# Query tiles transposed by VectorE in 32x32 blocks instead of by TensorE, tokens of a tile in another order, logits copied by ScalarE

## The chip, the cores and the metric

The kernel runs on one core of a Trainium2 chip. The core has five engines, each of which runs its own program in order: TensorE (PE, matrix products, with its weight loads shown as PEld), VectorE (DVE), ScalarE (ACT), GpSimd (POOL) and SyncE (SP, which here only issues DMAs). They meet through semaphores. Data are moved by 16 DMA engines. The metric is the device time of one execution in microseconds (us), smaller being better.

## The reference: what is computed

A multi-query attention (8 batches, 16 query heads, one key and value head, 384 tokens, head size 64) whose output, reshaped to 3072 tokens of 1024, goes through a mixture of experts with two levels of gates: a group of four, and in it one of four experts. Each token is handled by one expert of 16.

```python
scores = scale * np.matmul(q, k.transpose(0, 1, 3, 2))
attn = softmax(scores)                       # over the keys
x = np.matmul(attn, v)                       # -> (8*384, 16*64)
g_idx = np.argmax(x @ w_group, axis=1)
# for each group g and expert e of it:
e_idx = np.argmax(xg @ w_expert[g], axis=1)
h = np.maximum(xg[mask_e] @ w1[g, e], 0.0)
ye = h @ w2[g, e]
out[tok_idx] = (g_w * e_w)[:, None] * ye
```

With the inputs used, all 384 tokens of a batch go to one expert in seven batches; in the last batch 363 go to one and 21 to another.

## The kernel before

**Tiles and slots.** The 384 tokens of a batch are three tiles of 128 tokens; there are 24 tiles. In the kernel before, partition p of tile j holds token 3p + j. The 16 heads of a tile are eight pairs, called units. One pass of the main loop (`for i in range(NSL)`) is here called a slot. A slot handles two units, so a tile has 4 slots and a batch 12, and the loop has 96. The order of the work is written out by hand: nothing is rescheduled, each engine gets its instructions in the order in which the Python code issues them. `at(slot, where, fn)` puts a step into a slot, and `run(i, where)` calls it at that place of the slot.

**One slot**, in the order of issue: the scores of two units on PE (L161, two heads beside each other in the array, 8 matmuls; the scores fill both buffers of the pool `ps_s`); `soft`: for each unit the negated row maxima on DVE (L169, `nmx`) and two exponentials on ACT (L172, `pr`); then, in the first two slots of a tile (p = 0 and 1), small matmuls and groups of the expert's matmuls (`advance`), and in the last two (p = 2 and 3) half of the product with v of the tile before (L209); the places "v" and "m2"; two transposes on DVE in blocks of 32x32 (L193, into `ring`) of the probabilities of two slots before; the place "w"; the reciprocals of the row sums on DVE (L183, `rinv`), by which POOL scales the probabilities (L187); the place "g", where loads are issued. L209 reads the whole ring of a tile, and the last transposes of a tile stand in slot p = 1 of the next.

**Queries.** `load_q` brings a tile as 128 tokens x 16 heads x 64 by one DMA on SP, into one of three buffers. `q_group` turns four head pairs with four PE transposes against an identity (L147) into a bank of PSUM, which ACT copies to `qt` (L151). The second half of a tile is turned in its own slot p = 0, the first half of the next in slot p = 1.

**Gates.** After the attention of a tile, its logits are a matmul (L230, place "m2" of slot p = 0), copied to `lt` (L239, place "w"), summed by a second matmul in the next slot (L247) and copied to `lg` (L251, place "v"). `gate_masks` (L267 to L284, DVE and one exponential on ACT) runs behind the lg copy, also in "v", twice for a batch: for its first tile and for the other two. Slots are counted here from the first of the batch whose gates are meant, so that the numbers run on into the next batch's scores: lg copies stand in slots 9, 13 and 17 and the masks in 9 and 17. In slot 9 a small matmul (L294, `gate_choose`) counts the first tile's choices, from which the batch's expert is picked (`gate_pick`, slot 10), and its weights are loaded by POOL (L394).

**Experts.** The expert of a batch is 14 groups of 8 matmuls and an eviction: eight of the first layer (L419, evicted by ACT at L425 to `h_t`) and six of the second (L433, evicted at L451 to `y`). They are spread over slots p = 0 and 1 of the next batch: two groups in a slot, three in most slots p = 1, from slot 17 on. The three tiles of y are stored by SP (L476). The last batch has a second expert, whose results are stored in halves (L492). At the end a loop would handle any further pairs of batch and expert; there is none with these inputs.

Of the kernel before, what the change touches and what calls it, by code (L numbers as in the profile page):

```python
# [9 lines left out]
FP32 = mybir.dt.float32  # L10
BF16 = mybir.dt.bfloat16
I32 = mybir.dt.int32
P = 128
AX = mybir.AxisListType
ALU = mybir.AluOpType
# [4 lines left out]
def kernel(  # L20
# [11 lines left out]
    nc = tc.nc  # L32
# [15 lines left out]


    xb_dram = nc.dram_tensor("xb_scratch", [B, P, KO * S], BF16).ap()  # L50
    out_v = out.rearrange("(b p j) d -> b p j d", p=P, j=ST)
    w1f = moe_w1.rearrange("g e (ko ki) f -> (g e) ki ko f", ki=P)
    w2f = moe_w2.rearrange("g e (fo fi) d -> (g e) fi fo d", fi=P)

# [29 lines left out]
    ring = singles.tile([P, 3, 4, 2, S], FP32)  # L84
    NB = S // 32

    def xbank():
        x = ps_x.tile([P, 512], FP32, tag="x", name="x")
        return x
# [5 lines left out]

    def load_q(t, first=False):
        b, j = t // ST, t % ST
        q_sb = qpool.tile([P, H, D], FP32, tag="q", bufs=3)
        qv = q[b].rearrange("h (p j) d -> p j h d", j=ST)
        if first:  # L100
            nc.sync.dma_start(out=q_sb[:, 0:H // 4, :], in_=qv[:, j, 0:H // 4, :])
            nc.scalar.dma_start(out=q_sb[:, H // 4:H // 2, :], in_=qv[:, j, H // 4:H // 2, :])
            nc.sync.dma_start(out=q_sb[:, H // 2:H, :], in_=qv[:, j, H // 2:H, :])
        else:
            nc.sync.dma_start(out=q_sb[:], in_=qv[:, j, :, :])
        st["q", t] = q_sb

    def load_k(b, first=False):
# [29 lines left out]
    def q_group(t, half, parts=1):  # L138
        q_sb = st["q", t]
        half ^= swapped(t)  # L140
        qt = pool.tile([P, 512], FP32, tag="qt", bufs=3)
        n = 4 // parts
        for part in range(parts):
            pt = xbank()
            for c in range(part * n, (part + 1) * n):
                h = 2 * (half * 4 + c)
                nc.tensor.transpose(  # L147
                    out=pt[:, ts(c, P)], in_=q_sb[:, h:h + 2, :].rearrange("p t d -> p (t d)"), identity=ident[:]
                )
            r = slice(part * n * P, (part + 1) * n * P)  # L150
            nc.scalar.copy(out=qt[:, r], in_=pt[:, r])  # L151
        st["qt", t, half] = qt

    def scores(u):
# [26 lines left out]
    def norm(us):  # L181
        rinv = ppool.tile([P, 2, 2], FP32, tag="rinv")
        nc.vector.reciprocal(out=rinv[:], in_=st.pop(("ssum", us[0]))[:])  # L183
        for k, u in enumerate(us):
            for h in range(2):
                pr = st["pr", u][:, h, :]
                nc.gpsimd.tensor_scalar(  # L187
                    out=pr, in0=pr, scalar1=rinv[:, k, h:h + 1], scalar2=1.0, op0=ALU.mult, op1=ALU.mult
                )
# [46 lines left out]

    def logits_out(b, j):
        lt = pool.tile([P, P], FP32, tag="lt")
        nc.vector.tensor_copy(out=lt[:], in_=st.pop(("lt_ps", b, j))[:, 0:P])  # L239
        if j == 0:  # L240
            st["lg", b] = pool.tile([P, ST, NL], FP32, tag="lg", name="lg")
        st["lt", b, j] = lt
# [5 lines left out]
        st["l_ps", b, j] = l_ps  # L248

    def logits2_out(b, j):  # L250
        nc.vector.tensor_copy(out=st["lg", b][:, j, :], in_=st.pop(("l_ps", b, j))[:, 0:NL])  # L251


    NG = ST * (1 + G)
# [216 lines left out]
    def main_expert(b, on_act):  # L471
        w1, w2 = st.pop(("w", b))

        def store(j, y):
            if b < B - 1:
                nc.sync.dma_start(out=out_v[b, :, j, :], in_=y[:])  # L476
            else:
                st["y", j] = y

        yield from expert(st["xb", b], w1, w2, scaled(lambda: st["gsel", b][0], store), any_bank, on_act)  # L480

    def second_expert(on_act):

        b = B - 1

        def result(j, nh, yp, by_act):
            y = st["y", j]
            nc.vector.scalar_tensor_tensor(
                out=y[:, ts(nh, 512)], in0=yp, scalar=st["gsel", b][1][:, j:j + 1], in1=y[:, ts(nh, 512)],
                op0=ALU.mult, op1=ALU.add,  # L490
            )
            nc.sync.dma_start(out=out_v[b, :, j, ts(nh, 512)], in_=y[:, ts(nh, 512)])  # L492

        yield from expert(st["xb", b], *st.pop("w_second"), result, any_bank, on_act)

# [20 lines left out]
    def at(slot, where, fn, *args):  # L516
        later.setdefault((slot, where), []).append((fn, args))

    def run(slot, where):
        for fn, args in later.pop((slot, where), []):  # L520
            fn(*args)
# [36 lines left out]
            at(s0 + 8, "m0", prep_batch, b + 1)  # L558
            at(s0 + 8, "v", prep_out, b + 1)
    for t in range(NT):  # L560
        at(4 * t, "m1", q_group, t, 1)
        if t + 1 < NT:
            at(4 * t + 1, "m1", q_group, t + 1, 0)
        if 1 <= t < NT - 2:
            at(4 * t, "g", load_q, t + 2)

    load_k(0, first=True)
# [31 lines left out]
    busy(1)  # L599
    q_group(0, 0, 2)  # L600
    load_v(0)
    load_q(2)
    for i in range(NSL):
        t, p = i // 4, i % 4
        if i >= SB + 5 and (i - 5) % SB == 0:
            pending.append(main_expert((i - 5) // SB - 1, lambda k: True))
        us = (2 * i, 2 * i + 1)
        for u in us:
            scores(u)
        run(i, "s")  # L610
        soft(us, lambda: run(i, "b"))
        if p < 2:
            run(i, "m0")
            advance(1)
            run(i, "m1")
            advance(2 if p == 1 and t % ST > 0 else 1)
        elif t > 0:
            pv(t - 1, (p - 2) * NB // 2, (p - 1) * NB // 2)
        run(i, "v")
        run(i, "m2")  # L620
        if i >= 2:
            transp(2 * i - 4)
            transp(2 * i - 3)
        run(i, "w")
        norm(us)
        if p == 3 and t > 0:
            pv_out(t - 1)
        run(i, "g")
# [79 lines left out]
    with tc.For_i(0, n_rem, 1) as it:  # L708
        free.clear()
        e = nc.gpsimd.value_load(lse[0:1, ds(it, 1)], min_val=0, max_val=GE - 1)  # L710
        w1, w2 = load_w(e, 0), load_w(e, 1)
        bi = nc.sync.value_load(lsb[0:1, ds(it, 1)], min_val=0, max_val=B - 1)
        xr = pool.tile([P, KO, S], BF16, tag="xb", name="xr", bufs=2)
        nc.sync.dma_start(
            out=xr[:].rearrange("p c t -> p (c t)"), in_=xb_dram[ds(bi, 1)].rearrange("o p c -> (o p) c")
        )
        pid = nc.vector.value_load(lsi[0:1, ds(it, 1)], min_val=0, max_val=NP - 1)
        gcol = pool.tile([P, ST], FP32, tag="gcol")
        nc.vector.tensor_copy(out=gcol[:], in_=grem_all[:, ds(pid, 1), :].rearrange("p o j -> p (o j)"))
        bp = nc.gpsimd.value_load(lsb[0:1, ds(it, 1)], min_val=0, max_val=B - 1)  # L720

        def add(j, y):
            nc.gpsimd.dma_start(
                out=out_v[ds(bp, 1), :, j, :].rearrange("o p d -> (o p) d"), in_=y[:], accum_op=ALU.add
            )

        for _ in expert(xr, w1, w2, scaled(lambda: gcol, add), bank_end):
            pass
# [30 lines left out]
```

## Time and profile before

| | |
|---|---|
| median of 3 runs | 558.66 us (555.86 to 561.7) |
| profiled execution | 560.02 us, span of the profile 558.6 us |
| PE busy | 530.6 us, 95% of the span |
| DVE busy | 418.4 us, 75% |
| ACT busy | 339.2 us, 61% |
| POOL busy | 270.6 us, 48% |
| PE transposes of queries (L147) | 192, 29.5 us busy |
| their copies on ACT (L151) | 49, 29.0 us busy, 0.60 us for one of 128x512 |
| lt copies on DVE (L239) | 24, 6.7 us busy, 31.7 us of waiting ahead of them |
| lg copies on DVE (L251) | 24, 4.0 us busy |

The page is one profiled execution. A row of its groups names the line, the engine, the operation, and what is written from what, with the shape; behind it the busy time, the mean of one in ns, and the idle time of the engine ahead of it with what ended that. The chain is followed back from the last instruction to whatever released it, so its shares say which engine's work sets the end. In a timeline the first two numbers are start and length in us; "x4" says that several instructions are merged. The granted clock is the share of full speed that PE's clock was given.

### The profile page before, as it was taken

How to read it: one execution, taken by the hardware profiler on the slowest of the kernel's cores; microseconds unless marked ns; L12 is line 12 of the kernel's file. 1: busy time of each engine (PE TensorE's matmuls, PEld its weight loads, DVE VectorE, ACT ScalarE, POOL GpSimd, SP SyncE). 2: the span in 40 equal slices, each digit the busy share in tenths (PEclk: the TensorE clock that was granted, in tenths of full speed). 3: DMA queues.
4: the chain of work that ended last, by engine and by line, in shares of the span. 5: the costliest groups of instructions: out<-in, count | busy, mean ns of one | idle time of the engine just before them, and what ended most of it. 6: DMA issues, size and time to landing. Idle time of an engine off the chain costs nothing.

```text
span 558.6 us, 17530 instructions
## 1 busy us (share of the span) xinstructions
PE 530.6 (95%) x7074; PEld 310.1 (56%) x7074; DVE 418.4 (75%) x847; ACT 339.2 (61%) x1043; POOL 270.6 (48%) x456
## 2 busy tenths in 40 slices
PE   7598899999999999999999999999999999979994
PEld 3255456655665556655665556655665555555452
DVE  4989988877888778877888678876888778823322
ACT  4776666666666666766666676676666676613210
POOL 2655954564457444565447535555447535622000
PEclk9999999999999999999999999999999999989999
DMA  7710993099805993099706992199706960299923
GB/s 118 161 30 13 177 229 75 2 195 233 202 2 97 210 250 77 4 200 247 181 1 111 213 262 48 11 211 247 164 2 111 213 189 2 29 212 263 222 51 115
DMA packets 98098, 75.15 MB, mean 135 GB/s; under 512 B 75104, under 2 KB 75104, under 8 KB 98016
## 3 DMA queue, kind: packets, MB, share of 16 engines
q0 software_dynamic: 19008, 37.75, 38.1%
q1 hardware_dynamic: 78080, 36.04, 24.7%
q8 instruction: 57, 0.93, 0.7%
q10 hardware_dynamic: 928, 0.23, 0.2%
q14 instruction: 25, 0.20, 0.1%
HBM read 92.88 MB, written 18.87 MB: 200 GB/s over the span
## 4 chain that ended last, share of the span: by engine, by line
PE 88%; DVE 6%; ACT 3%; issue 2%; ACTq 0%; DVEq 0%
PE x L209 24%; PE s L161 22%; PE x L419 13%; PE x L433 11%; PE sb L433 6%; PE sb L419 4%; PE x L147 3%; DVE nmx L169 3%; ACT pr L172 3%; PE x L230 2%; DVE ring L193 2%; PE x L247 1%; PE x L94 1%; PE x L129 0%; PE x L338 0%
## 5 line engine op out<-in xcount | busy, mean ns | idle before, releaser
L187 POOL TENSOR_SCALAR pr<-pr,rinv 128x384 f32<-128x384 f32 x384 | 218.2, 591 | 222.6 <-DVE rinv L183 222.6
L172 ACT ACTIVATE pr<-s,nmx 128x384 f32<-128x384 f32 x384 | 217.9, 580 | 139.6 <-DVE nmx L169 133.1
L169 DVE TENSOR_REDUCE nmx<-s 128x2 f32<-128x768 f32 x192 | 174.4, 948 | 58.0 <-PE s L161 57.8
L193 DVE STREAM_TRANSPOSE ring<-pr 128x768 f32<-128x768 f32 x192 | 175.4, 952 | 0.0
L161 PE MATMUL s<-kt,qt 64*128 64x384 f32 x768 | 152.8, 511 | 13.0 <-ACT pr L172 12.8
L209 PE MATMUL x<-ring,v_sb 32*64 32x256 f32 x4608 | 142.5, 382 | 5.8 <-issue 4.8
L209 PEld LDWEIGHTS x<-ring,v_sb 32*64 32x64 f32 x4608 | 103.5, 132 | 47.8 <-issue 28.9
L161 PEld LDWEIGHTS s<-kt,qt 64*128 64x128 f32 x768 | 65.1, 186 | 71.5 <-ACT pr L172 37.3
L419 PE MATMUL x<-xb,w 128*128 128x384 bf16 x448 | 79.5, 326 | 0.0
L172 ACT ACTIVATION_READ_ACCUMULATOR pr<-s,nmx 128x1 f32 x384 | 77.9, 203 | 0.0
L419 PEld LDWEIGHTS <-w 128*128 128x128 bf16 x576 | 56.6, 100 | 32.0
L433 PEld LDWEIGHTS <-h_t 128*128 128x128 bf16 x432 | 41.3, 100 | 50.4 <-issue 9.1
L433 PE MATMUL x<-w,h_t 128*128 128x512 bf16 x288 | 68.2, 379 | 0.0
L222 ACT COPY xt<-x 128x256 f32<-128x256 f32 x96 | 29.1, 391 | 13.5 <-PE x L209 13.1
L425 ACT ACTIVATE h_t<-x 128x384 bf16<-128x384 f32 x56 | 28.2, 506 | 9.4 <-PE x L419 8.8
L433 PE MATMUL sb<-w,h_t 128*128 128x512 bf16 x144 | 33.2, 388 | 0.0
L394 POOL DMA_DIRECT2D w<-in_moe_w_dram x36 | 27.5, 777 | 10.5 <-PE x L247 5.6
L151 ACT COPY qt<-x 128x512 f32<-128x512 f32 (+1 forms) x49 | 29.0, 594 | 2.7 <-PE x L147 2.7
L239 DVE COPY lt<-x 128x128 f32<-128x128 f32 x24 | 6.7, 278 | 31.7 <-PE x L230 31.6
L147 PE MATMUL x<-ident,q_sb 128*128 128x128 f32 x192 | 29.5, 277 | 0.0
L147 PEld LDWEIGHTS x<-ident,q_sb 128*128 128x128 f32 x192 | 23.7, 143 | 8.9 <-issue 1.6
L223 POOL CAST xb<-xt 128x1024 bf16<-128x1024 f32 x24 | 24.9, 1040 | 7.5 <-ACT xt L222 7.5
(83 smaller groups left out, 217.5 us busy)
## 6 DMA issues: line engine op xcount, KB each, us to landing
w<-in_moe_w_dram POOLq DMA_DIRECT2D x36, 1024.0 KB, 18.7
q_sb<-in_q_dram SPq DMA_DIRECT2D x23, 512.0 KB, 6.4
out_dram<-y SPq DMA_DIRECT2D x21, 512.0 KB, 8.3
xb_scratch<-xb SPq DMA_DIRECT2D x8, 768.0 KB, 5.5
v_sb<-in_v_dram SPq DMA_DIRECT2D x32, 96.0 KB, 4.2
out_dram<-y SPq DMA_DIRECT2D x6, 256.0 KB, 2.0
kk<-in_k_dram SPq DMA_DIRECT2D x15, 96.0 KB, 5.4
q_sb<-in_q_dram SPq DMA_DIRECT2D x1, 256.0 KB, 4.1
```

Source lines behind the costliest of these rows:

```text
L147: nc.tensor.transpose(out=pt[:, ts(c, P)], in_=q_sb[:, h:h + 2, :].rearrange("p t d -> p (t d)"), identity=ident[:])
L151: nc.scalar.copy(out=qt[:, r], in_=pt[:, r])
L161: nc.tensor.matmul(out=s[:, h, 0:S], lhsT=qt[r, ts(cc, P)], rhs=kt[r, :], start=True, stop=True)
L169: nc.vector.tensor_reduce(out=nmx[:], in_=s[:, :, 0:S], axis=AX.X, op=ALU.max, negate=True)
L172: nc.scalar.activation(out=pr[:, h, :], in_=s[:, h, 0:S], func=ACTF.Exp, bias=nmx[:, h:h + 1], scale=1.0, accum_out=ssum[:, k, h:h + 1],)
L187: nc.gpsimd.tensor_scalar(out=pr, in0=pr, scalar1=rinv[:, k, h:h + 1], scalar2=1.0, op0=ALU.mult, op1=ALU.mult)
L193: nc.vector.transpose(out=ring[:, (u // 4) % 3, u % 4].rearrange("p h s -> p (h s)"), in_=st.pop(("pr", u))[:].rearrange("p h s -> p (h s)"),)
L209: nc.tensor.matmul(out=o[i][h * D:(h + 1) * D, 0:2 * P].rearrange("d (g c q) -> d g c q", g=2, c=4), lhsT=v_sb[r, n, :], rhs=ring[r, a:z + ...
L222: nc.scalar.copy(out=xt[:, :, ts(i, 32)], in_=o[:, 0:2 * P].rearrange("p (c q) -> p c q", c=KO))
L419: nc.tensor.matmul(out=hp[:, 0:S], lhsT=w1[:, ko, ts(fc, P)], rhs=xb[:, ko, :], start=(ko == 0), stop=(ko == KO - 1))
L425: nc.scalar.activation(out=h_t[:, fc, :], in_=hp[:, 0:S], func=ACTF.Relu)
L433: nc.tensor.matmul(out=yp, lhsT=h_t[:, fo, ts(j, P)], rhs=w2[:, fo, ts(nh, 512)], start=(fo == 0), stop=(fo == FO - 1),)
```

## The change

Five things are changed together.

- Which 128 tokens make a tile, and where they stand: tile j is now tokens 128j to 128j + 127, and partition 32n + r holds token 128j + 4r + n. The stores of the result follow: their destination has the dimensions n, r and d. Keys and values are as before.
- Tiles 0 to 4 are still turned by PE, but loaded in four DMAs, one for each n (tile 0 in eight, half of them on ACT's queue).
- Tiles 5 to 23 are loaded in four DMAs, one for each half of the 64 elements of each of two heads of a pair, with runs of 224 elements, of which blocks of 32 in every 64 are used. A new function, `q_blocks`, turns four pairs in one 32x32 block transpose on DVE, straight into `qt`. It stands at a new place "e", behind the reciprocals of the slot, in the same slots as `q_group`.
- The buffers of the queries are two of 2048 elements in each partition instead of three of 1024. The load of tile 2 moves from ahead of the loop to slot 0.
- The copies to `lt` and `lg` are issued to ACT instead of DVE, at the same places.

```diff
--- before.py
+++ after.py
@@ -48,7 +48,8 @@
 
 
     xb_dram = nc.dram_tensor("xb_scratch", [B, P, KO * S], BF16).ap()
-    out_v = out.rearrange("(b p j) d -> b p j d", p=P, j=ST)
+    QN = P // 32
+    out_v = out.rearrange("(b j r n) d -> b j n r d", j=ST, n=QN, r=32)
     w1f = moe_w1.rearrange("g e (ko ki) f -> (g e) ki ko f", ki=P)
     w2f = moe_w2.rearrange("g e (fo fi) d -> (g e) fi fo d", fi=P)
 
@@ -84,6 +85,8 @@
     ring = singles.tile([P, 3, 4, 2, S], FP32)
     NB = S // 32
 
+    TQ = 5
+
     def xbank():
         x = ps_x.tile([P, 512], FP32, tag="x", name="x")
         return x
@@ -95,14 +98,25 @@
 
     def load_q(t, first=False):
         b, j = t // ST, t % ST
-        q_sb = qpool.tile([P, H, D], FP32, tag="q", bufs=3)
-        qv = q[b].rearrange("h (p j) d -> p j h d", j=ST)
-        if first:
-            nc.sync.dma_start(out=q_sb[:, 0:H // 4, :], in_=qv[:, j, 0:H // 4, :])
-            nc.scalar.dma_start(out=q_sb[:, H // 4:H // 2, :], in_=qv[:, j, H // 4:H // 2, :])
-            nc.sync.dma_start(out=q_sb[:, H // 2:H, :], in_=qv[:, j, H // 2:H, :])
+        q_sb = qpool.tile([P, 2 * H * D], FP32, tag="q", bufs=2)
+        if t < TQ:
+            q_sb = q_sb[:, 0:H * D].rearrange("p (h d) -> p h d", h=H)
+            qv = q[b].rearrange("h (j r n) d -> j n r h d", n=QN, r=32)
+            for h0 in range(0, H, H // 2 if first else H):
+                for n in range(QN):
+                    (nc.scalar if first and n % 2 else nc.sync).dma_start(
+                        out=q_sb[32 * n:32 * (n + 1), h0:h0 + (H // 2 if first else H), :],
+                        in_=qv[j, n, :, h0:h0 + (H // 2 if first else H), :],
+                    )
         else:
-            nc.sync.dma_start(out=q_sb[:], in_=qv[:, j, :, :])
+
+            q_sb = q_sb[:].rearrange("p (c x) -> p c x", c=H // 2)
+            qv = q[b].rearrange("(c h) (j r n) d -> h j r c (n d)", h=2, n=QN, r=32)
+            for i in range(4):
+                nc.sync.dma_start(
+                    out=q_sb[32 * i:32 * (i + 1), :, 0:QN * D - 32],
+                    in_=qv[i // 2, j, :, :, 32 * (i % 2):32 * (i % 2) + QN * D - 32],
+                )
         st["q", t] = q_sb
 
     def load_k(b, first=False):
@@ -149,6 +163,14 @@
                 )
             r = slice(part * n * P, (part + 1) * n * P)
             nc.scalar.copy(out=qt[:, r], in_=pt[:, r])
+        st["qt", t, half] = qt
+
+    def q_blocks(t, half):
+
+        half ^= swapped(t)
+        qt = pool.tile([P, 512], FP32, tag="qt", bufs=3)
+        q_sb = st["q", t][:, 4 * half:4 * (half + 1), :].rearrange("p c (n d) -> p (c n) d", n=QN)
+        nc.vector.transpose(out=qt[:].rearrange("p (x d) -> p x d", d=32), in_=q_sb[:, :, 0:32])
         st["qt", t, half] = qt
 
     def scores(u):
@@ -236,7 +258,7 @@
 
     def logits_out(b, j):
         lt = pool.tile([P, P], FP32, tag="lt")
-        nc.vector.tensor_copy(out=lt[:], in_=st.pop(("lt_ps", b, j))[:, 0:P])
+        nc.scalar.copy(out=lt[:], in_=st.pop(("lt_ps", b, j))[:, 0:P])
         if j == 0:
             st["lg", b] = pool.tile([P, ST, NL], FP32, tag="lg", name="lg")
         st["lt", b, j] = lt
@@ -248,7 +270,7 @@
         st["l_ps", b, j] = l_ps
 
     def logits2_out(b, j):
-        nc.vector.tensor_copy(out=st["lg", b][:, j, :], in_=st.pop(("l_ps", b, j))[:, 0:NL])
+        nc.scalar.copy(out=st["lg", b][:, j, :], in_=st.pop(("l_ps", b, j))[:, 0:NL])
 
 
     NG = ST * (1 + G)
@@ -473,7 +495,7 @@
 
         def store(j, y):
             if b < B - 1:
-                nc.sync.dma_start(out=out_v[b, :, j, :], in_=y[:])
+                nc.sync.dma_start(out=out_v[b, j], in_=y[:])
             else:
                 st["y", j] = y
 
@@ -489,7 +511,7 @@
                 out=y[:, ts(nh, 512)], in0=yp, scalar=st["gsel", b][1][:, j:j + 1], in1=y[:, ts(nh, 512)],
                 op0=ALU.mult, op1=ALU.add,
             )
-            nc.sync.dma_start(out=out_v[b, :, j, ts(nh, 512)], in_=y[:, ts(nh, 512)])
+            nc.sync.dma_start(out=out_v[b, j, :, :, ts(nh, 512)], in_=y[:, ts(nh, 512)])
 
         yield from expert(st["xb", b], *st.pop("w_second"), result, any_bank, on_act)
 
@@ -558,10 +580,12 @@
             at(s0 + 8, "m0", prep_batch, b + 1)
             at(s0 + 8, "v", prep_out, b + 1)
     for t in range(NT):
-        at(4 * t, "m1", q_group, t, 1)
-        if t + 1 < NT:
-            at(4 * t + 1, "m1", q_group, t + 1, 0)
-        if 1 <= t < NT - 2:
+        for x, u, half in ((4 * t, t, 1), (4 * t + 1, t + 1, 0)):
+            if u < TQ:
+                at(x, "m1", q_group, u, half)
+            elif u < NT:
+                at(x, "e", q_blocks, u, half)
+        if t < NT - 2:
             at(4 * t, "g", load_q, t + 2)
 
     load_k(0, first=True)
@@ -599,7 +623,6 @@
     busy(1)
     q_group(0, 0, 2)
     load_v(0)
-    load_q(2)
     for i in range(NSL):
         t, p = i // 4, i % 4
         if i >= SB + 5 and (i - 5) % SB == 0:
@@ -623,6 +646,7 @@
             transp(2 * i - 3)
         run(i, "w")
         norm(us)
+        run(i, "e")
         if p == 3 and t > 0:
             pv_out(t - 1)
         run(i, "g")
@@ -721,7 +745,7 @@
 
         def add(j, y):
             nc.gpsimd.dma_start(
-                out=out_v[ds(bp, 1), :, j, :].rearrange("o p d -> (o p) d"), in_=y[:], accum_op=ALU.add
+                out=out_v[ds(bp, 1), j].rearrange("o n r d -> (o n) r d"), in_=y[:], accum_op=ALU.add
             )
 
         for _ in expert(xr, w1, w2, scaled(lambda: gcol, add), bank_end):
```

## The prediction

> **What bounds the kernel now.** I read the profile page first (parts 1, 2 and 4), then the chain in order of time, then the timeline of the same stretch.
>
> ```profile
> PE 530.6 (95%) x7074; PEld 310.1 (56%) x7074; DVE 418.4 (75%) x847; ACT 339.2 (61%) x1043; POOL 270.6 (48%) x456
> ...
> PE 88%; DVE 6%; ACT 3%; issue 2%; ACTq 0%; DVEq 0%
> ```
>
> TensorE (PE) carries 88% of the chain that ended last. A slot, one pass of the loop over two head pairs, looks so in the chain (start, length, what):
>
> ```profile
> 262.71 1.49 PE s L161 x8
> 264.20 0.34 PE x L247 x2
> 264.54 1.30 PE x L419 x8
> 265.84 0.44 PE x L147 x4
> 266.28 2.60 PE x L419 x16
> 268.88 1.49 PE s L161 x8
> 270.37 2.78 PE x L209 x96
> 273.15 1.49 PE s L161 x8
> ```
>
> From scores to scores PE does not wait. The four query transposes (L147) are 0.44 us on it. The other engines in this slot (a gate slot, the 18th of a batch):
>
> ```profile
> 265.35 0.17 DVE L251 COPY lg<-x 128x20 f32<-128x20 f32 x1
> 265.55 0.20 DVE L267 TENSOR_REDUCE mx<-lg 128x10 f32<-128x40 f32 x1
> ...
> 266.89 1.83 DVE L193 STREAM_TRANSPOSE ring<-pr 128x768 f32<-128x768 f32 x2
> ...
> 268.92 0.49 ACT L425 ACTIVATE h_t<-x 128x384 bf16<-128x384 f32 x1 [0.65 <-PE x L419]
> ...
> 269.77 1.82 DVE L169 TENSOR_REDUCE nmx<-s 128x2 f32<-128x768 f32 x2 [1.00 <-PE s L161]
> ...
> 270.83 0.58 ACT L172 ACTIVATE pr<-s,nmx 128x384 f32<-128x384 f32 x1 [1.29 <-DVE nmx L169]
> ```
>
> VectorE (DVE) copies lg as soon as PE has it and goes straight on to the gates and to the ring, which PE's L209 needs next. ScalarE (ACT) ends the slot only after PE's last expert matmul: its third h_t starts at 268.92, 0.04 us behind it.
>
> **What goes.** 19 of 24 tiles lose two groups of L147: 38 x 0.44 = **-16.7 us**, all on the chain. ACT loses 38 copies of 0.60 us, off the path.
>
> **What comes on DVE.** 38 block transposes of 128x512. The nearest row, the ring's, moves 128x768 at a pitch of 0.91: 0.61 by size, 0.63 taken. The source is read in runs of 32 elements, which no row shows: 1.27 is the upper bound (half rate), 0.49 the lower (half the 0.95 of a ring instruction). They stand behind rinv and ahead of the next maxima. In a slot without gates DVE then has 1.82 + 1.83 + 0.14 + 0.63 = 4.4 us in a PE slot of 5.3 to 5.7: covered. PE waits for none, as the scores use the result two slots later or at the next tile. DVE loses the 24 lt copies, which held it waiting for PE; in the first tiles, where DVE is on the chain, I count -0.8 in all.
>
> **What moves: the lg copy.** The lt copy on ACT costs nothing: ACT idles 1.8 us there before its next exponentials. The lg copy does. In ACT's program it stands behind the slot's four exponentials and its expert evictions, three in a gate slot, and the third waits for PE's last matmul. DVE is in order, so its gate reduction L267 now waits for that, and the ring transposes, rinv, the block transpose and the next maxima wait behind it. This happens in slots 9 and 17 of a batch (counted from 0); the other lg copies have no early reader.
>
> Slot 17, in the times above: PE's fill ends at 268.44. Third h_t 268.48 to 268.97; lg copy about 0.2 (the 128x20 exponential on ACT took 0.22) to 269.17; L267 at 269.25 instead of 265.55; gates 1.34 (265.55 to 266.89); ring 270.59 to 272.42. PE has finished its scores at 269.93 and L209 waits until 272.56: **2.63 us idle**. DVE: rinv and block transpose to 273.19, then maxima; exponentials 1.06 after their start, at 274.25. Early in the trace, where PE waits for score banks, scores start 1.29 and 2.41 us after the first exponential (8.75 to 10.04 and 11.16). So the next scores start at 275.54 and 276.66, L209 runs to 280.19, and the following scores end at 281.68 instead of 278.90: 2.78 late with the 0.44 already credited, **3.2 us** gross. Seven times: +22.4.
>
> Slot 9: PE's own gate_choose matmul (L294) needs the mask. Fill ends 288.94; lg done 289.67; mask 290.9; L294 at 291.1, **2.15 us idle** on PE; scores to 292.73; ring to 292.72; maxima 293.6; exponentials 294.68; scores 295.97 and 297.09; then gate_pick (0.91) on DVE; scores of the next tile end at 302.50 instead of 299.53, 3.4 gross. ACT is then so late that two evictions and the lt copy end at 308.6, where PE wants lt at 308.1: 0.6 more. **4.0 us**, seven times: +28.0. In batch 0 slot 9 has no expert: lg would come at 45.9 instead of 43.7, +1.9.
>
> **Ends.** Tile 0 arrives in eight DMAs on two queues; the last of its first half is issued about 0.8 us later than now (SP takes 0.8 for one): +0.6. load_q(2) moves past SP's small loads into slot 0 and lands (6.4 us median) long before slot 5. Each later tile is four issues on SP instead of one, and with two buffers it waits for the tile's second block transpose; four slots (20 us) remain against 6.4 (21.3 at most): nothing counted. In the tail lg waits behind an eviction: +0.5.
>
> Sum so far: -16.7 + 22.4 + 28.0 + 1.9 - 0.8 + 1.1 = **+35.9**.
>
> **The clock.** PE's idle stretches have a second price. Columns: stretch, length, PE busy, ..., granted clock, DMA share, GB/s.
>
> ```profile
> 13.12:16.54 3.42, 1.83 (x8) 0.60 (x8) 1.95 (x4) 2.81 (x10) 2.25 (x5) 1.00 0.82 186
> ...
> 494.40:497.82 3.42, 1.43 (x47) 0.93 (x32) 0.00 (x0) 0.00 (x0) 1.27 (x2) 1.00 1.08 270
> 497.82:504.64 6.82, 5.89 (x63) 3.30 (x63) 0.00 (x0) 1.29 (x4) 1.04 (x1) 0.50 1.12 212
> ```
>
> After 3.42 us with 1.99 idle the clock was halved for 6.82 us; after 3.42 with 1.59 idle it was not. I read this as a fixed grid of 3.41 us and a limit between, 1.8. An idle 2.63 puts 1.8 into one interval from 72% of the starting points, 2.15 from 57%: 7 x 0.72 + 7 x 0.57 = 9 halvings. In slot 17 one makes L209 and the scores take twice their time until about 279.3, and the following scores end some 2.8 us later: 25. Part is given back where PE would have waited anyway: 0.4 and 0.6 in slot 9's sum, and 0.7 in slot 8, where DVE has 6.1 us against PE's 5.4, 1.7 x 7 = 12. **+13.5.**
>
> The Trainium skill (TensorE: Matmul & The Clock Gate, Part 1: The HAM clock gate) says the clock halves after at least one idle window of about 3.4 us. A 2.6 us wait alone would then do nothing and the time would be that of the rival without halvings. The row above, halved after 1.43 us of work in the window, speaks against it.
>
> Total +49.4 on the profiled execution's 560.02 us (span 558.6 and 1.4 around it), which is 1.4 above the median of 558.66: **608 us**.
>
> **Rivals.**
> - *No halvings*: +35.9, 594.5 us. For it: one row carries the price. Chance 0.22.
> - *The output stores become narrow*: the destination was one dimension of 128 rows and is now 4 x 32. In the last 15 us a 256 KB store takes 0.74 us at a DMA share of 0.92, 0.74 x 0.92 x 16 = 10.9 us of one engine. On 4 engines that is 2.7, six stores one behind the other from 544.63 end 16.3 later instead of at 552.28: +8.7, 617 us. No row shows such a store. The Trainium skill (DMA: Bandwidth & Descriptors, Why a DMA increments its semaphore by 16 and not by 1) says that the number of engines must divide the slowest dimension of both sides, which gives 4 here. Chance 0.20.
> - *Dear block transposes* (1.27): +0.64 in 14 chains and as much in slot 8 seven times, +13, 621 us. Chance 0.08.
> - *Faster*: the gates wait less than thought. The two stalls pay for the gain as soon as one costs 16.7 / 14 = 1.2 us; if DVE's lg came before ACT's evictions, only -16.7 and small terms stay: 542 us. Against it: both engines run their programs in order, and the eviction ahead of lg ends after PE's fill. Chance 0.05.
> - *The new token order changes the routing*: from the inputs, seven batches send all 384 tokens to one expert and the last 363 and 21 to two, so the first tile picks the same in either order. A further expert would be 20.8 us (520.43 to 541.19). With late query loads: 0.03.
>
> The forecast itself has 0.42. Range **590 to 622**: from no halvings with cheap transposes (-2) and 2 of noise, to narrow stores with a few halvings more. A difference under 1% can't be told from none in this kernel. Faster by over 1% 0.05, within 1% 0.02, slower 0.93.
>
> **What would show it.** Right: L267 waits 14 times for ACT's lg, 3 to 4 us each; L209 waits for the ring; granted clock below 0.97; slots of plain tiles 0.44 shorter; block transposes near 0.63. Wrong: L267 starting right behind the second maximum, or a PE that stays busy through slots 9 and 17.

## The result: slower, 611.7 us

The changed kernel takes **611.7 us** (median of 6 runs, 607.67 to 612.79) against 557.64 us for the kernel before, now also of 6 runs: a ratio of 1.0946, 95% interval 1.0894 to 1.0997. Its profiled execution took 608.54 us, its span is 607.0 us against 558.6, and the mean granted clock is 0.964 against 0.991. The time is 3.7 us above the forecast of 608 and inside the range. The sum behind the forecast was less right than its end: it priced the main loop 14.8 us too high and the tail 14.1 us too low. The experiments below show where.

From the page of the changed kernel, its engines, the chain by engine, two groups and the weights' loads:

```profile
PE 532.5 (88%) x6900; PEld 302.4 (50%) x6922; DVE 430.2 (71%) x837; ACT 328.5 (54%) x1053; POOL 269.9 (44%) x456
...
PE 62%; DMA 12%; DVE 10%; ACT 6%; issue 4%; POOL 2%; SPq 1%; POOLq 0%; DVEq 0%; ACTq 0%
...
L289 DVE TENSOR_REDUCE mx<-lg 128x5 f32<-128x20 f32 (+1 forms) x16 | 3.0, 185 | 68.6 <-ACT lg L273 68.6
...
L173 DVE STREAM_TRANSPOSE qt<-q_sb 128x512 f32<-128x512 f32 x38 | 26.0, 683 | 0.0
...
w<-in_moe_w_dram POOLq DMA_DIRECT2D x36, 1024.0 KB, 21.9
```

PE has 152 weight loads fewer, those of the query transposes, and is busy a little longer all the same, as a part of its work ran at half clock. Its share of the chain fell from 88% to 62%. Two things took its place. DVE's gate reduction (L289, formerly L267) waits 68.6 us for ACT's copy of lg, which was expected; and 12% of the chain is now DMA (7% loads of weights, 5% loads of keys), which was not: the median weight load takes 21.9 us from issue to landing instead of 18.7. The block transposes take 683 ns each.

The chain of the changed kernel in slot 17 of a batch, the place that the prediction worked out (start, length, what):

```profile
416.39 3.90 PE x L441 x24
420.29 1.49 PE s L183 x8
421.78 2.41 issue
424.19 3.18 PE x L231 x94
427.37 1.64 PE s L183 x8
```

There is no L161 (formerly L147) left, and PE stands still for 2.41 us between the scores and the product with v. The timeline of the same place, ACT, DVE and PE, says why:

```profile
420.33 0.49 ACT L447 ACTIVATE h_t<-x 128x384 bf16<-128x384 f32 x1 [0.70 <-PE x L441]
420.71 0.17 ACT L273 COPY lg<-x 128x20 f32<-128x20 f32 x1
420.92 0.20 DVE L289 TENSOR_REDUCE mx<-lg 128x10 f32<-128x40 f32 x1 [3.64 <-ACT lg L273]
...
422.25 1.83 DVE L215 STREAM_TRANSPOSE ring<-pr 128x768 f32<-128x768 f32 x2
...
424.07 0.68 DVE L173 STREAM_TRANSPOSE qt<-q_sb 128x512 f32<-128x512 f32 x1
424.19 0.68 PE L231 MATMUL x<-ring,v_sb 32*64 32x256 f32 x8 [2.41 <-issue]
```

PE had lg's matmul ready at 416.39. ACT copies it at 420.71, behind the third eviction (L447), which waits for PE's last expert matmul. DVE has waited 3.64 us; gates and ring follow, and L231 starts when the ring is done. The list of waits of the whole execution (in total, times, longest):

```profile
DVE mx L289 <- ACT lg L273: 68.6, 16, 17.1
...
PE x L316 <- DVE g_mask L306: 15.8, 8, 2.7
```

One of the 16 waits, of 17.1 us, lies in the tail; the other 15 have a mean of (68.6 - 17.1) / 15 = 3.4 us.

To see where the time went, I take the span apart at two points: the first scores, and the first scores of the last slot.

| us | first scores | loop | tail | span |
|---|---|---|---|---|
| before | 6.79 | 474.2 | 77.6 | 558.6 |
| after | 7.14 | 507.7 | 92.2 | 607.0 |
| difference | +0.35 | +33.5 | +14.6 | +48.4 |

The tail, that is everything behind the start of the last slot's scores, lost 14.6 us, where the prediction counted 0.5. Its waits for DMAs in the changed kernel:

```profile
ACT y L473 <- DMA out_dram<-y: 3.6, 1, 3.6
...
PEld L441 <- DMA w<-in_moe_w_dram: 3.5, 1, 3.5
PE sb L441 <- DMA w<-in_moe_w_dram: 3.2, 1, 3.2
PE sb L455 <- DMA w<-in_moe_w_dram: 3.0, 1, 3.0
```

The kernel before had none of these. PE waits twice: at 555.86 for the second-layer weights of the last batch's expert, at 571.10 for the first-layer weights of the second expert (the PEld row is the same wait as the PE row below it). With each wait the clock is halved for 3.41 us, from 556.67 and from 570.32. The load behind the second wait is the longest piece of the chain:

```profile
527.02 44.03 DMA w<-in_moe_w_dram
```

In the kernel before the same load took 30.5 us, and PE did not wait for it. And when DVE has written the last result at 593.45, the output is not nearly out. The windows of the changed kernel at that point, while results still come and after the last one (stretch, length, PE, PEld, DVE, ACT, POOL, granted clock, DMA share, GB/s):

```profile
586.00:593.50 7.50, 6.66 (x31) 2.84 (x29) 3.54 (x5) 0.00 (x0) 0.00 (x0) 1.00 0.25 78
594.00:604.00 10.00, 0.00 (x0) 0.00 (x0) 0.00 (x0) 0.00 (x0) 0.00 (x0) 0.68 0.25 95
```

and the same stretch of the kernel before, up to its last result:

```profile
545.00:552.40 7.40, 6.55 (x31) 2.75 (x29) 3.43 (x5) 0.00 (x0) 0.00 (x0) 1.00 0.41 158
```

The DMA share stands at 0.25, as much as four engines of 16, for 17 us. The last six stores are 768 packets with a mean of 93 ns; they take 18.0 us from the first packet to the last, so 768 x 0.093 / 18.0 = 4.0 engines work on the average. From 586 us on, exactly four packets are under way for 12.2 us of 18.2; in the kernel before, the last stores have up to 16 at a time. This is the rival of the narrow stores, and the Trainium skill's rule that the prediction cited for it (DMA: Bandwidth & Descriptors, Why a DMA increments its semaphore by 16 and not by 1) agrees with these rows.

### The profile page after: what moved, and what is told of

Its sections match the earlier page's. It is cut to its first block, busy times and chain, and to the rows that moved or that the text cites. A ratio compares the mean times of both kernels' runs of the same rounds, so it can differ in the third digit from the quotient of the medians.

```text
span 607.0 us, 17318 instructions
## 1 busy us (share of the span) xinstructions
PE 532.5 (88%) x6900; PEld 302.4 (50%) x6922; DVE 430.2 (71%) x837; ACT 328.5 (54%) x1053; POOL 269.9 (44%) x456
## 4 chain that ended last, share of the span: by engine, by line
PE 62%; DMA 12%; DVE 10%; ACT 6%; issue 4%; POOL 2%; SPq 1%; POOLq 0%; DVEq 0%; ACTq 0%
PE x L231 19%; PE s L183 17%; PE x L441 10%; PE x L455 9%; DMA w<-in_moe_w_dram 7%; DMA kk<-in_k_dram 5%; ACT pr L194 5%; DVE nmx L191 4%; DVE ring L215 3%; PE sb L441 2%; PE sb L455 2%; PE x L252 2%; POOL pr L209 1%; PE x L269 1%; SPq L125 1%
## 5 line engine op out<-in xcount | busy, mean ns | idle before, releaser
L183 PE MATMUL s<-kt,qt 64*128 64x384 f32 x768 | 158.0, 521 | 13.6 <-ACT pr L194 12.4
L231 PE MATMUL x<-ring,v_sb 32*64 32x256 f32 x4608 | 151.1, 397 | 20.7 <-issue 16.8
L231 PEld LDWEIGHTS x<-ring,v_sb 32*64 32x64 f32 x4608 | 113.1, 138 | 63.5 <-issue 48.3
L441 PE MATMUL x<-xb,w 128*128 128x384 bf16 x448 | 76.2, 326 | 0.0
L455 PE MATMUL x<-w,h_t 128*128 128x512 bf16 x270 | 64.3, 380 | 0.9
L289 DVE TENSOR_REDUCE mx<-lg 128x5 f32<-128x20 f32 (+1 forms) x16 | 3.0, 185 | 68.6 <-ACT lg L273 68.6
L447 ACT ACTIVATE h_t<-x 128x384 bf16<-128x384 f32 x56 | 26.0, 500 | 10.2 <-PE x L441 9.6
L473 ACT ACTIVATE y<-x,gsel 128x512 f32<-128x512 f32 x36 | 24.2, 696 | 3.7 <-PE x L455 3.7
L173 DVE STREAM_TRANSPOSE qt<-q_sb 128x512 f32<-128x512 f32 x38 | 26.0, 683 | 0.0
L441 PE MATMUL sb<-xb,w 128*128 128x384 bf16 x128 | 22.9, 339 | 3.2 <-DMA w<-in_moe_w_dram 3.2
## 6 DMA issues: line engine op xcount, KB each, us to landing
w<-in_moe_w_dram POOLq DMA_DIRECT2D x36, 1024.0 KB, 21.9
```

Of the source, the lines that this page charges most:

```text
L173: nc.vector.transpose(out=qt[:].rearrange("p (x d) -> p x d", d=32), in_=q_sb[:, :, 0:32])
L183: nc.tensor.matmul(out=s[:, h, 0:S], lhsT=qt[r, ts(cc, P)], rhs=kt[r, :], start=True, stop=True)
L231: nc.tensor.matmul(out=o[i][h * D:(h + 1) * D, 0:2 * P].rearrange("d (g c q) -> d g c q", g=2, c=4), lhsT=v_sb[r, n, :], rhs=ring[r, a:z + ...
L441: nc.tensor.matmul(out=hp[:, 0:S], lhsT=w1[:, ko, ts(fc, P)], rhs=xb[:, ko, :], start=(ko == 0), stop=(ko == KO - 1))
L447: nc.scalar.activation(out=h_t[:, fc, :], in_=hp[:, 0:S], func=ACTF.Relu)
L455: nc.tensor.matmul(out=yp, lhsT=h_t[:, fo, ts(j, P)], rhs=w2[:, fo, ts(nh, 512)], start=(fo == 0), stop=(fo == FO - 1),)
```

## Experiments

Each time is a median, with its ratio to the kernel before run on the same chip (557.4 to 557.9 us). "Loop" and "tail" are as in the table above.

| run | us | ratio, 95% interval | loop | tail |
|---|---|---|---|---|
| after | 611.7 | 1.0946 (1.0894 to 1.0997) | 507.7 | 92.2 |
| e1_lg_dve | 580.03 | 1.0387 (1.0356 to 1.0417) | 482.3 | 92.0 |
| e2_lg_act_only | 612.62 | 1.0995 (1.0963 to 1.1027) | 525.3 | 75.6 |
| e3_wide_store | 594.85 | 1.0640 (1.0596 to 1.0683) | 513.4 | 75.5 |
| e4_both | 542.51 | 0.9711 (0.9683 to 0.9740) | 459.9 | 77.3 |
| e5_fill | 586.12 | 1.0522 (1.0490 to 1.0554) | 501.8 | 75.7 |
| e6_narrow_only | 557.67 | 1.0001 (0.9984 to 1.0017) | 472.9 | 75.9 |
| e7_pe_transposes | 562.05 | 1.0087 (1.0057 to 1.0117) | 477.2 | 75.2 |
| e8_lg_early | 559.52 | 1.0052 (1.0028 to 1.0076) | 473.4 | 76.5 |
| e9_narrow_only2 | 580.14 | 1.0406 (1.0357 to 1.0454) | 480.8 | 90.4 |
| e10_wide_last | 605.53 | 1.0897 (1.0828 to 1.0967) | 509.0 | 85.8 |

### The lg copy: undone, and alone

e1_lg_dve is the changed kernel with one line taken back:

```diff
-        nc.scalar.copy(out=st["lg", b][:, j, :], in_=...)
+        nc.vector.tensor_copy(out=st["lg", b][:, j, :], in_=...)
```

> The changed kernel with one line undone: the lg copy is issued to VectorE again. In the changed kernel's profile the loop from the first scores to the last slot's takes 507.7 us against 474.2 before, and what follows the last slot's first scores 92.2 against 77.6. Wait theory (gates wait for the lg copy behind the evictions): slots 9, 10, 18 and 19 of every batch fall back, and the loop loses the 16.7 us of the PE transposes against before, so about 458; the end stays as it is; about 559 us in all. Rival, load theory (the block transposes, 26.0 us of VectorE, are what makes the loop late): the loop stays above 490 and the time above 590.

e2_lg_act_only is the kernel before with only this line changed, in the other direction.

> The kernel before with one line changed: the lg copy is issued to ScalarE. Everything else, the PE transposes too, is as before. Wait theory: slots 9 and 17 of a batch cost 3 to 4 us each, 14 of them, and one in batch 0: about 50 us in the loop, and some halvings of PE's clock with a us or two each; 610 us. Load theory: VectorE only loses 4.0 us of work; 555 to 560 us.

**Measured:** e2 takes 612.62 us. One line of 24 copies of 0.17 us costs 54.8 us, as much as the whole change. Its waits:

```profile
DVE mx L267 <- ACT lg L251: 61.3, 16, 4.3
```

e1 takes 580.03 us: 31.7 less than the changed kernel, but not the 559 of the wait theory alone. Its gate slots are as short as they should be; something else is late. The waits of e1, and its chain in slot 8 of a batch:

```profile
PE x L143 <- DMA kk<-in_k_dram: 15.4, 5, 3.5
```

```profile
268.59 1.80 SPq L125
270.39 0.05 issue
270.44 15.26 DMA kk<-in_k_dram
285.70 0.14 issue
285.84 0.88 PE x L143 x3
```

A load of the keys, 96 KB, needs 15.26 us from issue to landing; its median before was 5.4. Slot 8 is 5.80 us long in the kernel before and 8.4 to 11.7 in five batches of e1. And the tail is as long as in the changed kernel. Both point at the DMAs.

### The stores

e3_wide_store is the changed kernel with each store issued as four, one for each n, 32 rows each. e4_both has this and lg on DVE.

```diff
-                nc.sync.dma_start(out=out_v[b, j], in_=y[:])
+                for n in range(QN):
+                    nc.sync.dma_start(out=out_v[b, j, n], in_=y[32 * n:32 * (n + 1), :])
...
-            nc.sync.dma_start(out=out_v[b, j, :, :, ts(nh, 512)], in_=y[:, ts(nh, 512)])
+            for n in range(QN):
+                nc.sync.dma_start(out=out_v[b, j, n, :, ts(nh, 512)], in_=y[32 * n:32 * (n + 1), ts(nh, 512)])
```

> The changed kernel with each store of the result issued as four DMAs of 32 rows (n = 0 to 3) instead of one of 4 x 32 rows; the same bytes. In the changed kernel the last 2 KB packets end 10.7 us after the last result is written to its buffer, before it was 2.9. Narrow-store theory: this falls to about 3 us, and PE's two waits for the last weights (2.97 and 3.17 us, each with a half-speed stretch behind it) go or shrink, as the stores ahead of them no longer hold a few DMA engines: 12 to 15 us less, about 597 us. Rival: the weights are late for another reason (larger query loads, another start): only the 7 to 8 us at the very end go, about 604 us, and the two waits stay.

> Both edits together: lg copy on VectorE and stores in four DMAs. If the wait theory and the narrow-store theory both hold, what is left is the gain of 16.7 us less small terms at the start: about 543 us, faster than before by 2.5%. By the load theory still above 575.

**Measured:** 594.85 and **542.51 us**. In e3 the waits for weights in the tail are gone, the longest weight load there takes 31.7 us instead of 44.0, and the tail is 75.5 us. e4 is 2.9% faster than the kernel before and the fastest of all. So these two edits together take back 611.7 - 542.5 = 69.2 us, more than the whole loss. They overlap: lg costs 594.85 - 542.51 = 52.3 us with wide stores and 31.7 with narrow ones; the stores cost 37.5 us with lg on DVE and 16.9 with lg on ACT. With lg on ACT the price of the stores is the tail's alone (92.2 us against 75.5). In e1 PE waits 15.4 us in all for keys; in the changed kernel, where it waits for the gates before, only 0.7: there the late loads have time to land.

e10_wide_last widens only the last six stores and leaves the 21 in the loop narrow.

> The changed kernel with only the last tile's six stores of 256 KB (columns halved) as four times 32 rows; the 21 stores of 512 KB in the loop stay as the changed kernel has them. If the tail's loss is the last stores' own time on few engines: the last bytes come 10.7 us earlier (they ended 10.7 behind the last result of 593.45), less 2.9 as before, 8 to 11 us faster than 611.7, 601 to 604 us, with the two waits for the last weights (2.97 and 3.17 us) still there. If these stores only queue behind earlier ones: no gain, 609 to 612. As much as is then left to 594.85 is the loop's stores'.

**Measured:** 605.53 us, a little above the expected 601 to 604. From the last result to the end of the span it is now 7.6 us instead of 13.6; from the last slot's scores to the last result it is still 78.2 us (78.6 after, 67.4 in e3), and the waits for the weights are there (3.0, 2.6 and 2.4 us). So about 6 us of the tail's loss is the last stores' own time. The larger part, 78.2 - 67.4 = 10.8 us against e3, goes only when the earlier stores are wide too: it is the waits for weights and what follows them.

### The narrow destination alone

e6_narrow_only and e9_narrow_only2 are the kernel before with another view of the output, e6 with n outside r, e9 with the changed kernel's; the stores' index follows.

```diff
-    out_v = out.rearrange("(b p j) d -> b p j d", p=P, j=ST)
+    out_v = out.rearrange("(b j n r) d -> b j n r d", j=ST, n=P // 32, r=32)   # e6
+    out_v = out.rearrange("(b j r n) d -> b j n r d", j=ST, n=P // 32, r=32)   # e9
```

> The kernel before with the changed destination of the output stores alone: rows of a store 4 x 32 in the output, as in the changed kernel, while the tokens of a tile stay as they were, so the rows of the output stand in another order than the reference's. Everything else is the kernel before. With lg on VectorE the narrow stores cost 37.5 us in the changed kernel (580.03 against 542.51), 14.4 of them in the tail, the rest in waits for the keys' and values' loads in slot 8 of five batches. If the stores alone hold those loads: tail and waits together, 585 to 597 us. If it takes the query loads in quarters beside them (four issues on SP for one): the tail's 14.4 alone, 572 us.

> The kernel before with the changed kernel's view of the output, the order of the 128 rows of a store being 4 with a step of one row inside 32 with a step of four rows, so that no two dimensions of it lie behind one another (where the 32 rows of one group lie side by side, as in the run of that name without the 2, a store took 8.2 us, like the 8.3 of before, and the time stayed 557.67). Everything else is the kernel before; the rows of the output stand in another order than the reference's. If the stores alone hold the loads of keys, values and weights, as they seem to with lg on VectorE (580.03 against 542.51): tail and waits together, 585 to 597 us. If it takes the query loads in quarters beside them: the tail's 14.4 alone, 572 us. If the stores cost nothing and only the block transposes' loads do: 558 us.

**Measured:** e6 takes 557.67 us, no different from the kernel before. I had chosen it badly: with n outside r the 128 rows lie behind one another, the four groups of 32 are again one run of 128 rows with one step, and a store takes 8.2 us from issue to landing as before (8.3). It shows that a view of four dimensions alone costs nothing. e9, where the dimensions can't be joined, takes 580.14 us: 22.7 more, and again in both places, +12.8 in the tail and +6.6 in the loop. In the loop it is mostly the queries that come late, in slot 5 of six batches (6.52 to 7.46 us long instead of 6.17). Its chain in the tail holds one piece of DMA:

```profile
501.88 41.65 DMA w<-in_moe_w_dram
543.53 0.05 issue
543.58 9.92 PE sb L419 x60
```

This weight load takes 41.65 us here, where the kernel before needed 30.5; PE waits for it and works without a gap afterwards. The 580.14 lies between my two readings (585 to 597, and 572). The tail's loss is the stores' alone: everything else is the kernel before. The loop's loss is 6.6 us with the old query loads and 482.3 - 459.9 = 22.4 in e1 against e4, where queries come in four loads of short pieces and slots are shorter. Which of those two makes the difference wasn't separated.

### The halved clock

e5_fill is e3 with eight matmuls of zeros in each of PE's two waits. The same edit goes into `gate_choose`, into its bank `c_ps`.

```diff
             st["o", t] = [xbank() for _ in range(P // 32)]
+            for _ in range(8 if t % ST == 0 else 0):
+                nc.tensor.matmul(out=st["o", t][0][:], lhsT=blank[:, 0:P], rhs=blank[:], ...)
```

> The changed kernel with stores of four times 32 rows (594.85 us), and in each of its two waits of a batch eight matmuls of zeros on PE, 128x512, some 0.22 us each at full clock by the 0.47 that they take at half clock at the start of the trace: ahead of the first product with v of a batch's first tile, and ahead of the matmul that gate_choose makes. They write the bank that the next matmul overwrites, so nothing is computed otherwise. They fill about 1.7 of the 2.2 to 2.4 us that PE waits there and delay nothing, if the wait is longer than they are. Theory that the halved clock comes from PE's idle time in one interval of 3.41 us: the four halvings in the loop go, each of which makes a slot 1.5 to 1.8 us longer in that kernel's trace (8.84 and 8.76 against 7.07, 5.88 against 4.34), 588 us, and none is seen in the loop behind the first batch. Rival, the halvings have another cause: they stay, 594 to 596 us.

**Measured:** 586.12 us, 8.7 less, by giving PE more work. The timeline of PE in slot 17, with the filler at L227, and the windows of the stretch from 24.28 to 580.65:

```profile
414.24 1.56 PE L183 MATMUL s<-kt,qt 64*128 64x384 f32 x8
415.74 1.90 PE L227 MATMUL x<-blank 128*128 128x512 bf16 x8
418.16 3.17 PE L233 MATMUL x<-ring,v_sb 32*64 32x256 f32 x96 [0.52 <-DVE rinv L205]
```

```profile
24.28:580.65 556.37, 534.32 (x6987) 301.10 (x6985) 413.43 (x776) 315.58 (x1016) 260.64 (x434) 1.00 0.66 143
```

The wait itself is as long as before: from the scores' end to the product with v it is still about 2.4 us, of which 1.90 are filled. The clock is never halved in these 556 us. The affected slots are 7.02 and 8.04 us long, as in the undisturbed batches of the changed kernel (7.07 and 8.10). So it is PE's idle time that halves the clock here, and the waits themselves are the larger part of the price: e5 is still 43.6 us above e4. The 8.7 us are not the price of the filled places' halvings alone. In the two profiles the loop of e5 is 11.6 us shorter than e3's; 5.6 of these come from slot 7 of the second batch (10.26 us against 4.67), which has a wait of another kind and no filler. And in slot 6 of the first batch, where PE does not wait, the filler itself costs 1.8 us (6.58 against 4.75).

The windows of the changed kernel around two halvings and around a wait that caused none (columns as above; all in the grid of 3.41 us on which the clock changes):

```profile
242.64:246.05 3.41, 1.40 (x10) 0.85 (x10) 2.31 (x8) 0.78 (x3) 0.00 (x0) 1.00 0.21 35
246.06:249.47 3.41, 3.41 (x46) 1.64 (x50) 3.41 (x7) 1.24 (x5) 2.26 (x4) 0.50 0.02 5
287.02:290.43 3.41, 1.00 (x13) 0.42 (x12) 3.24 (x11) 0.24 (x1) 0.14 (x1) 1.00 0.35 127
290.43:293.84 3.41, 3.41 (x69) 3.41 (x71) 3.41 (x5) 2.19 (x8) 2.12 (x4) 0.50 0.35 126
293.85:297.26 3.41, 3.41 (x77) 2.11 (x69) 1.79 (x4) 0.52 (x3) 2.27 (x4) 1.00 0.30 114
420.13:423.54 3.41, 1.65 (x9) 0.69 (x8) 2.45 (x9) 0.79 (x3) 0.00 (x0) 1.00 0.35 128
```

After 1.40 or 1.00 us of work in an interval the clock is halved for the next one; after 1.65 it is not. It comes back after one interval if PE was busy in it.

### The place of the copy, and the gain by itself

e8_lg_early is e3 with lg still on ACT, but its copy issued right behind its matmul, ahead of the slot's expert groups:

```diff
-            at(x + 1, "v", logits2_out, b, j)
+            at(x + 1, "m0", logits2_out, b, j)
```

> The changed kernel with stores of four times 32 rows (594.85 us); lg stays on ACT, but its copy is issued right behind PE's matmul for it, ahead of the slot's expert matmuls, so that in ACT's program it stands behind the four exponentials and ahead of the three evictions. Theory that the price is the place behind the evictions: lg comes about 1.1 us later than on VectorE (two exponentials of 0.58 behind the second maximum) instead of 3.7, the ring is done 0.5 us before PE's product wants it, and PE waits for neither: 543 to 548 us. Rival, the wait of VectorE for another engine's copy is itself the price, wherever it stands: 585 to 595 us.

**Measured:** 559.52 us, 35.3 less than e3 and 17.0 more than e4. Its waits:

```profile
DVE mx L289 <- ACT lg L273: 42.3, 16, 17.0
...
PE x L316 <- DVE g_mask L306: 3.4, 7, 1.7
```

Outside the tail DVE waits (42.3 - 17.0) / 15 = 1.7 us instead of 3.4. So two thirds of the price of the copy, 35.3 of 52.3 us, was its place behind the evictions. My 543 to 548 was wrong: 1.7 us late is not free. The chain in slots 20 and 21 of a batch (8 and 9 of the next) shows what binds then:

```profile
406.21 1.74 DVE ring L215 x2
407.96 0.06 DVE rinv L205
408.01 0.60 DVE qt L173
408.61 0.85 DVE nmx L191
409.50 0.04 issue
409.55 0.82 ACT pr L194 x3
410.37 0.22 issue
410.58 1.33 ACT pr L194 x5
411.91 0.07 ACT lg L273
412.01 0.19 DVE mx L289
```

No PE is in it, from 402.93 to 419.08: ring, block transpose, maximum, exponentials, lg, gates, all one behind the other on DVE and ACT. Here the block transpose is on the path too. A batch is some 2 us longer than in e4 (61.24 against 59.08 in the fifth).

e7_pe_transposes is e4 with `TQ = 24` in place of 5: no tile is transposed by blocks.

> The changed kernel with lg on VectorE and stores of four times 32 rows (542.51 us), but all 24 tiles as the first five: queries loaded in four DMAs of 32 tokens and transposed by PE (0.44 us a group, 38 groups) with the copy on ACT. No block transposes are left. If the block transposes are the whole gain over the kernel before: 542.5 + 16.7 = 559 us, no different from the kernel before (557.8). If part of the gain is the lt copy on ACT or the new order of tokens: between 543 and 557.

**Measured:** 562.05 us, 4.2 above the kernel before and 19.5 above e4. The block transposes are the whole gain. A single slot of e7, in its second batch, is 11.63 us long instead of 6.65, for a query load took 23.55 us; without those 5.0 us it would be at 557, if they come in its other executions too, which no trace shows. Expected was no difference from the kernel before.

## Why the prediction was right, and which of its terms were not

**The mechanism of the lg copy: right.** L289 waits for ACT's copy, 15 times in the loop at 3.4 us (3 to 4 predicted); PE's idle time in slot 17 was 2.41 us (2.63), in slot 9 15.8 / 8 = 2.0 (2.15). e1, e2 and e4 show that this line carries it.

**Queries off PE: right.** Plain slots are 0.44 us shorter each (6.06 to 5.62, 5.72 to 5.28, 6.17 to 5.73), and e7 shows that nothing else is gained. **Block transposes: right**, 0.68 us against 0.63 (the lower bound, half of 0.95, is 0.48 and not 0.49), and hidden wherever PE is the bound, as e4 shows. The dear one of 1.27 is excluded.

**The terms of the sum**, measured from slots that no halving touches (e3 against e4), from e5, and from the table above:

| term, us | predicted | measured |
|---|---|---|
| slot 17, seven times | 3.2 each, 22.4 | 2.95 each, 20.7 |
| slot 9, seven times | 4.0 each, 28.0 | 2.9 each, 20.3 |
| batch 0, slot 9 | 1.9 | 1.9 |
| clock, in the loop | 13.5 | about 9 |
| start | 0.6 | 0.35 |
| tail | 0.5 | 14.6 |

The 2.95 are slots 18 and 19 of a batch: 7.08 and 4.41 against 4.27 each. The 2.9 are 8.10, 4.34, 4.67 and 5.81 against 5.86, 4.27, 4.27 and 5.62. The clock's 9 are the slots of the changed kernel with a halving against those of e5: 2.4, 1.7, 1.1, 1.1, 1.5 and 1.1. The 1.9 of batch 0 are 8.41 (in e5, without a halving) against 6.53. With the -16.7, and the -0.4 seen in the first slots (-0.8 predicted), these make 35 for the loop, whose measured 33.5 also holds some us of a slot (the fourth of a batch) that varies, from the second batch on, between 4.27 and 5.70 over the kernels, the one before included.

The loop and the tail are those of the two profiled executions, 560.02 and 608.54 us, which differ by 48.5 us. The medians, 557.64 and 611.7, differ by 54.1. No trace shows where the other 5.6 us are.

**Slot 9, 1.1 us too dear.** The prediction put `gate_pick` (0.91) between the late scores and the next tile's, and 0.6 for evictions that ACT would be late with. Neither showed. Behind a slot 9 without a halving, the product with v of slot 11 starts at 451.49, right behind that slot's scores, and the next tile's scores end at 455.94, 13.05 us behind the end of the fill; the prediction had 13.56.

**The clock, 4.5 us too dear.** The limit of some 1.8 us idle, 1.6 of work, was near: 1.65 us of work stayed at full clock and 1.40 did not. Wrong were the length and the number. The one row of before showed 6.82 us, and I took it for every halving. In the loop of the changed kernel five of six are 3.41 us long and one is 6.83; and there were six, not nine. The Trainium skill's rule (TensorE: Matmul & The Clock Gate, Part 1: The HAM clock gate), which asks for an idle window, doesn't describe these rows: the windows that halved the clock held 1.00 and 1.40 us of work.

**The tail, 14.1 us too cheap.** The step that failed is the treatment of the stores as a rival, where it should have been a term beside the others. Nothing excluded that both happen, and both did: the stalls of the forecast and the four engines of the rival. The rival's +8.7 for the last stores was near: from the last result to the end it is 13.58 us instead of 6.24, +7.3, of which e10 takes back 6.0. But it left out the other half, +7.3 (78.6 us against 71.3 from the last slot's scores to the last result): narrow stores make loads late that run beside or behind them, the weights here, the keys in e1, the queries in e9. How they hold these loads up in detail no view shows. The parts of the forecast for the loop come to 48.3 us, against 33.5 measured, and for the tail to 0.5, against 14.6: the forecast came out near because the one paid for the other, and that is luck.

**The faster rival: wrong for this kernel, right about the price.** It named 542 us for a change without its stalls. e4 measures 542.51; its gain over its own kernel before is 15.3 us (557.80 to 542.51), where the rival had 16.7.

## What to carry to other kernels

A copy of 0.17 us is priced by what stands ahead of it in its new engine's program and by what waits behind it, not by its length: look for the reader, then count what the engine must finish first. When the order of rows in memory changes, look at every DMA that writes them: whether the rows still lie at one step made the difference between e6 (557.67 us) and e9 (580.14), and a narrow store is paid for by other loads too. And a rival that excludes nothing of the forecast belongs into the sum.

## What the runs showed of the hardware that was not expected

- **The clock's grid.** Halvings begin and end on multiples of 3.41 us from one another in each trace. I laid this grid over the twelve traces: some 1,900 intervals at full clock, of which 65 were followed by half clock. With less than 1.43 us of PE work in an interval half clock followed every time, between 1.43 and 1.81 it went either way, and above that the clock stayed, but for three intervals of 2.08 us in the first batch. At half clock, an interval with up to 2.55 us of work was followed by another at half clock, and one with 2.64 or more by full clock, with three exceptions (2.76, 3.31 and 3.37). So a halving lasts 3.41 us where PE is busy in it and 6.83 where it has another gap. What else than busy time decides in the exceptions is open.
- **Filling an idle PE with zeros** saved 8.7 us in a kernel whose waits could not be filled with anything useful, with no change to the waits (e5). A part of this, 5.6 us in the profiles, comes from a single slot without a filler, the one below.
- **One wait is not explained.** Slot 7 of the second batch is 4.27 us long in the kernel before and in e2, e6, e7 and e9, which have no block transposes. It is 4.67 in e5, 5.81 in the changed kernel, 5.67 to 8.08 in e1, e4, e8 and e10, and 10.26 in e3, with a halving of 6.83 us. In e4 PE stands still for 1.62 us in the middle of the scores, for nothing that the profile shows. It comes once in an execution. No run was made for it.
